# Five moves in the instruction order of a chunkwise mLSTM with an MLP on one core: sums, scans and x of two early steps, one weight chunk, and the low parts of the fourth tile

## The chip, the core and the metric

The kernel runs on one core of a Trainium2 chip. A core has five engines that run side by side, each with its own queue of instructions, which it takes in order: TensorE (PE) for matrix products, with its weight loads shown apart (PEld), VectorE (DVE), ScalarE (ACT), GpSimd (POOL), and SyncE (SP), which here does nothing but issue transfers (DMAs). The metric is the device time of one execution in microseconds (us). 

## What is computed

The reference is a recurrent attention layer (mLSTM) over 4 batches, 8 heads, 768 positions and 40 values a head, and an MLP over the 3072 tokens that come out, cut here to its core:

```python
for t in range(S):
    m_new = np.maximum(f_gate[:, :, t] + m, i_gate[:, :, t])
    f_stab = np.exp(f_gate[:, :, t] + m - m_new)
    i_stab = np.exp(i_gate[:, :, t] - m_new)
    C = f_stab * C + i_stab * (v_t outer k_t)
    n = f_stab * n + i_stab * k_t
    y[:, :, t] = sigmoid(o_t) * (C @ q_t) / max(|n . q_t|, 1)
x = y as tokens (3072 x 320)
h = x @ w_in                       # 320 x 2048
g = max(h, 0) + log1p(exp(-|h|))   # softplus
out = g @ w_out                    # 2048 x 320
```

The weights arrive as pairs of 32-bit words (float64) and are turned into float32 on the chip.

## The kernel before

**Steps and tiles.** The recurrence is worked in chunks of 128 positions. A chunk of one batch with its 8 heads is a *step*; there are 24, in the order of the list ORDER (line 35): the first chunks of all four batches as steps 0 to 3, then batch 0's chunks 1, 2 and 3 as steps 4, 5, 6, and so on. Three steps make a *tile* of 384 tokens, and there are 8 tiles, counted from 0. Names carry batch and chunk: x0_1 is x of batch 0, chunk 1 (step 4), pw0_2_0 the first half (4 heads) of step 5's decay matrix, X1 the tokens of tile 1; loq3 belongs to tile 3, the fourth.

**A step.** Steps 0 to 2 are written out in `first_tile`, steps 3 to 5 are run by `plain_step` (line 770), steps from 6 on by `wide_step` (line 832). The pieces of a step 3 to 5, in the order of the data: `decay`, a scan on DVE that makes the matrix of decays pw of four heads (L447), from factors fb that SP loads; `last_decays` (gw, L469) and `state_values` on POOL (vw, L475); `scores` (L517): PE's products of k and q into sp (L522), which DVE multiplies into pw (L524); `inter` (L543): the old state by q (ip, L546) and DVE's y1 (L549); `state` (cp, L499) and `new_state` (cn, L504); `values` (L553): PE's yp (L556), DVE's sum yy of yp and y1 (L560), its denominator nq (L562 to L564), POOL's product of the gate sig by it (L565), and DVE's x (L568); last `split_x` (L627): PE turns x over into xp (L633, L635), ACT casts it to a high part in X (L637), and DVE writes the low part (L639). `values` is a generator that is resumed by next(v): the first pieces up to POOL's product stand in the loop of `plain_step`, x is next(v) of line 823. From step 6 on the pieces have wide forms: iq (L575) and y (L578) on DVE, yq (L586), y again (L591), the transfer yd (L598), its reads yx and nw (L602 to L606), which POOL issues, and X.

**High and low parts.** PE multiplies in a rounded format, so operands are split into a high part (a cast) and a low part (the rest). For tiles from 2 on `prepare` (line 282) loads q and k of the three steps, ACT casts the high parts (hiq, hik, L300), and POOL makes the low parts (loq, lok) in two pieces of four heads each (L306). After each piece the generator waits for a number of products from the list PSY (L307, L309), [8, 12]: 8 for tile 2, 12 for later ones. SP then copies parts to the operands of a step: high parts by `load` (L391), low ones by `load_low` (L405), into qst and kst.

**Weights.** 16 chunks, eight (u, 0) of w_in and eight (u, 1) of w_out, each 256 of the 2048 columns or rows, run through `single` (line 204): two ACT instructions (mago or magi L212, sgo or sgi L215), two on DVE (L217, L219), then a cast to the high part on ACT (wih L250, woh L265) and the low part on POOL (wil L257, wol L267). `convert` (line 887) spaces these by the lists CW and CO, counted from a start that lines 1066 to 1072 set.

**The products.** For each tile and each of 16 blocks of 128 columns PE does 8 products hp (L1005, 384 columns), ACT two softplus passes (gh L877, hp L878), DVE the low part gl (L881), and PE, two blocks later, 9 products po (L971, 320 columns). ob (L1030, L1049) takes the results out; ob0h is a half result of tile 0, which is summed in two halves. X of a tile must be whole before its first hp block.

**What sets the order.** The products are written out in a fixed row, and everything else is put between them by a heap of generators (`start`, `resume`, `tick`, lines 917 to 940). A generator yields the number of products, counted from its own base, after which it wants to go on; a yield of -1000 - r means r products from now. For steps 3 to 5 these numbers are N_LOAD to N_XP (line 276), with bases 0, 40 and 76, for later steps W_LOAD to W_FIN (line 272). So a number smaller by 4 puts a piece four products sooner in the row of every engine that it uses. `in_order` (line 111) then pins on each engine the order in which the instructions were written. Small PSUM tiles (sp, cp, ip, yp, xp and their wide forms) take turns in two buffers (`Pair`, line 69), so the order of their use also sets who waits for whose buffer.

## Time and profile before

| | |
|---|---|
| median of three runs | 483.1 us (482.81 to 484.28) |
| the profiled execution | 484.25 us |
| span of its instructions in the trace | 482.5 us |
| TensorE busy | 466.4 us, 97% of the span |
| its weight loads, beside it | 445.2 us |
| VectorE busy | 325.0 us, 67% |
| ScalarE and GpSimd busy | 217.0 and 217.3 us, 45% each |
| mean clock granted to TensorE | 0.992 of full speed |

Busy time is time in which an engine had an instruction running; the span runs from the first instruction to the last. The profiled execution is one of its own, 1.15 us above the median of the runs, and 1.75 us of its time lie outside the span. In rows of the trace, a group of like instructions has its line, engine and operation, out<-in by the program's names with the numbers left out, shape and type of both, and how often it came (x); what stands in square brackets is the idle time of the engine just before, and the instruction or transfer that ended it ("issue" if the trace shows none). In a time line the first two columns are the start of a group in us and the time that it took. SPq and POOLq are the queues in which SP and POOL issue transfers.

### The profile page before, as it was taken

The numbers are of one execution on the slowest core, as the hardware profiler recorded it, in microseconds if no ns is written. First come the engines' busy times: TensorE is split into PE (matmuls) and PEld (weight loads), VectorE is DVE, ScalarE is ACT, GpSimd is POOL, SyncE is SP. The second block draws the span as 40 slices with busy tenths as digits, with TensorE's granted clock in tenths as the row PEclk, the third lists the DMA queues.
The fourth block names the chain that finished last, engine by engine and source line by source line (L and its number), as shares of the span: only waits on it lengthen the run. The fifth ranks groups of instructions, "written<-read, shape, count | busy, mean of one in ns | idle before, by whom it ended". The sixth has DMA issues, their size and how long they took to land.

```text
span 482.5 us, 9346 instructions
## 1 busy us (share of the span) xinstructions
PE 466.4 (97%) x3444; PEld 445.2 (92%) x3444; DVE 325.0 (67%) x517; ACT 217.0 (45%) x424; POOL 217.3 (45%) x303
## 2 busy tenths in 40 slices
PE   8999988998998999999999999999999999999996
PEld 7978887988898999999999999999999999999996
DVE  8879978778767768658757858767857856542121
ACT  1657536475744534354424434353425433334232
POOL 8366467477675145534275146525275244200000
PEclk9999998999999999999999999999999999999999
DMA  6957975789967984768667874669657461001001
GB/s 173 282 153 250 228 220 173 195 211 298 189 190 218 243 252 118 184 189 217 175 165 195 216 224 122 176 201 213 169 168 205 126 221 39 20 20 43 0 1 41
DMA packets 45607, 81.10 MB, mean 168 GB/s; under 512 B 6626, under 2 KB 23482, under 8 KB 45562
## 3 DMA queue, kind: packets, MB, share of 16 engines
q1 hardware_dynamic: 38218, 68.80, 52.1%
q0 software_dynamic: 4320, 8.26, 6.8%
q10 hardware_dynamic: 3024, 3.44, 2.1%
q8 instruction: 27, 0.44, 0.4%
q14 instruction: 18, 0.15, 0.1%
HBM read 52.38 MB, written 8.80 MB: 127 GB/s over the span
## 4 chain that ended last, share of the span: by engine, by line
PE 74%; DMA 13%; DVE 8%; issue 2%; SPq 2%; ACT 1%; DVEq 0%
PE hp L1005 32%; PE po L971 31%; PE yq L586 3%; DMA fb<-fz_d 3%; DMA wr<-in_w_in 3%; PE sp L522 3%; DVE pw L447 2%; PE cp L499 2%; DMA qst<-hiq 2%; PE iq L575 2%; DMA y<-fc_d 1%; DMA kst<-in_qk 1%; DMA sgp<-og 1%; DMA qst<-in_qk 1%; DVE sgo L219 1%
## 5 line engine op out<-in xcount | busy, mean ns | idle before, releaser
L1005 PE MATMUL hp<-X,wih 128*128 128x384 f32 x768 | 181.7, 341 | 0.4 <-ACT X L637 0.4
L877 ACT ACTIVATE gh<-hp 128x384 fp32r<-128x384 f32 x128 | 62.6, 489 | 160.0 <-PE hp L1005 142.2
L1005 PEld LDWEIGHTS hp<-X,wih 128*128 128x128 f32 x768 | 132.6, 189 | 2.2 <-issue 0.9
L881 DVE TENSOR_TENSOR gl<-hp,gh 128x384 fp32r<-128x384 f32 x128 | 70.1, 548 | 57.1 <-ACT hp L878 56.9
L971 PE MATMUL po<-woh,gh 128*128 128x320 f32 x384 | 83.7, 316 | 1.2 <-ACT ob0h L1030 1.2
L971 PE MATMUL po<-woh,gl 128*128 128x320 f32 x384 | 83.8, 313 | 0.0
L971 PE MATMUL po<-wol,gh 128*128 128x320 f32 x384 | 83.0, 316 | 0.0
L447 DVE TENSOR_TENSOR_SCAN pw<-fb,ident 128x512 f32<-128x512 f32 x48 | 72.4, 1545 | 4.1 <-DMA fb<-fz_d 3.6
L1005 PE MATMUL hp<-X,wil 128*128 128x384 f32 x256 | 69.1, 343 | 0.0
L971 PEld LDWEIGHTS po<-woh,gh 128*128 128x128 f32 x384 | 65.9, 190 | 2.3 <-ACT ob0h L1030 1.5
L971 PEld LDWEIGHTS po<-wol,gh 128*128 128x128 f32 x384 | 62.5, 190 | 1.6 <-issue 1.2
L971 PEld LDWEIGHTS po<-woh,gl 128*128 128x128 f32 x384 | 63.0, 189 | 0.3 <-issue 0.2
L878 ACT ACTIVATE hp<-hp 128x384 f32<-128x384 f32 x128 | 62.2, 486 | 0.0
L598 POOL DMA_DIRECT2D yd<-y x36 | 20.8, 578 | 90.4 <-DVE y L591 89.2
L1005 PEld LDWEIGHTS hp<-X,wil 128*128 128x128 f32 x256 | 45.8, 188 | 1.1 <-issue 1.0
L578 DVE TENSOR_TENSOR y<-iq,y 41x512 f32<-41x512 f32 x36 | 24.5, 682 | 29.5 <-PE iq L575 28.6
L522 PEld LDWEIGHTS sp<-qst,kst 120*128 120x128 f32 (+1 forms) x240 | 32.2, 191 | 5.7 <-issue 1.9
L522 PE MATMUL sp<-qst,kst 120*128 120x128 f32 (+1 forms) x240 | 33.1, 271 | 4.0 <-issue 1.7
L475 POOL TENSOR_TENSOR vw<-vt,gw 128x328 f32<-128x328 f32 x19 | 16.2, 854 | 39.3 <-DVE gw L469 27.5
L524 DVE TENSOR_TENSOR pw<-sp,pw 128x512 f32<-128x512 f32 x48 | 32.1, 682 | 1.7 <-PE sp L522 1.3
L623 ACT CAST X<-eg 128x384 fp32r<-128x384 f32 x18 | 9.2, 513 | 52.2 <-DVE eg L621 52.2
L504 DVE TENSOR_TENSOR cn<-cn,cp 40x328 f32<-40x328 f32 x16 | 7.8, 486 | 31.1 <-POOL cn L490 29.6
(131 smaller groups left out, 593.7 us busy)
## 6 DMA issues: line engine op xcount, KB each, us to landing
fb<-fz_d SPq DMA_DIRECT2D x42, 256.0 KB
vt<-in_vko SPq DMA_DIRECT2D x23, 324.0 KB
qst<-hiq SPq DMA_DIRECT2D x36, 160.0 KB
kst<-hik SPq DMA_DIRECT2D x36, 160.0 KB
wo<-in_w_out SPq DMA_DIRECT2D x8, 640.0 KB
wr<-in_w_in SPq DMA_DIRECT2D x8, 512.0 KB
eg<-in_oT SPq DMA_DIRECT2D x6, 576.0 KB
yd<-y POOLq DMA_DIRECT2D x36, 96.0 KB, 3.5
```

The lines of the kernel that those rows point to most:

```text
L447: nc.vector.tensor_tensor_scan(pw.rearrange(flat), fb.rearrange(flat), ident4.rearrange(flat), 0.0, ALU.mult, ALU.add)
L475: nc.gpsimd.tensor_tensor(z.vw, v1, z.gw.broadcast_to([128, H, E]), op=ALU.mult)
L522: nc.tensor.matmul(sp[:, j, :], z.kst[:, h, :], z.qst[:, h, :], start=True, stop=True)
L524: nc.vector.tensor_tensor(z.pws[i], sp, z.pws[i], op=ALU.mult)
L578: nc.vector.tensor_tensor(y, iq, y, op=ALU.mult)
L586: nc.tensor.matmul(yq[e0:e1, p, :], z.via[:, h * E : h * E + e1 - e0], z.pws[h // HG][:, h % HG, :], start=True, stop=True)
L598: nc.gpsimd.dma_start(rows[i], z.y[i * PP : i * PP + EP])
L877: nc.scalar.activation(gh, hp, AF.Softplus)
L878: nc.scalar.activation(hp, hp, AF.Softplus)
L881: nc.vector.tensor_tensor(gl, hp, gh, op=ALU.subtract)
L971: nc.tensor.matmul(po[j], a[:, j * 128 : (j + 1) * 128], w[:, f, :], start=(first and left[j] == 2), stop=(last and left[j] == 0),)
L1005: nc.tensor.matmul(hp, a, r, start=(i == 0), stop=(i == len(seq) - 1))
```

## The change

The edits, in the order of the diff:

- N_X and N_XP, the counts at which x is made and turned over, get one value for each of steps 3, 4 and 5. For step 3 x goes from 60 to 54 and now stands ahead of the parking of the state, its xp stays at 80; for step 4 x goes from 60 to 56 and xp from 72 to 64; step 5 keeps 60 and 72.
- PSY gets a value of its own for tile 3: 5 products between low parts in place of 12.
- In `split_x` the spacing of the cast and the low part behind xp becomes 2 and 3 products for step 3 and 1 and 1 for steps 4 and 5; before it was 2 and 3 for steps 3 and 4, and 1 and 1 for step 5.
- In `plain_step` the scan of the second half, before done apart for step 4 alone, is done apart for steps 4 and 5, and its place is now given as a count. For step 5 the first half's scan comes behind the matrix products of the first scores, just ahead of the product that reads it, and not ahead of them.
- The state copy of step 8 (`stack`, cs, L323 and L324) is due 12 products later, its scans 14 later (-30 to -16).
- The last piece of w_out chunk 6 (its low part) is due at 25 in place of 22 and w_in chunk 5 starts 9 products later.

The order of SP's instructions stays the same. Lines behind 784 of the kernel stand 8 further on in the changed one: L971, L1005 and L881 of the kernel before are L979, L1013 and L889 there.

```diff
--- before.py
+++ after.py
@@ -274,7 +274,7 @@
         -48, -34, -64, -8, 19, 8, 4, 6, 14, 17, 31, 47, 50, 62, -12, 68, 79, 107, 139,
     )
     N_LOAD, N_FB, N_SCAN, N_CN, N_VW, N_SIG, N_SP0, N_SP1, N_CP, N_CD, N_IP, N_VI, N_YP, N_X, N_XP = (
-        -20, -22, 9, 26, 12, 12, 12, 24, 40, 44, 45, 30, 46, 60, 72,
+        -20, -22, 9, 26, 12, 12, 12, 24, 40, 44, 45, 30, 46, (54, 56, 60), (80, 64, 72),
     )
     OF = [0, 8]
     N_PARK = 57
@@ -304,9 +304,9 @@
             for h in range(0, H, 4):
                 h2 = slice(h, h + 4)
                 nc.gpsimd.tensor_tensor(lo[:, h2], lo[:, h2].bitcast(F32), hi[:, h2], op=ALU.subtract)
-                yield -1000 - PSY[t > WIDE]
-
-    PRD, PSY = [62, 38, 78], [8, 12]
+                yield -1000 - PSY[min(t - WIDE, 2)]
+
+    PRD, PSY = [62, 38, 78], [8, 5, 12]
 
     parts = {}
     Xs = {}
@@ -633,9 +633,9 @@
             nc.tensor.transpose(xp[:, j, :], z.x[:, j * L : (j + 1) * L], ident)
         for j in range(2):
             nc.tensor.matmul(xp[j * 64 : (j + 1) * 64, 2, :], z.x[:, 2 * L :], ident, start=True, stop=True)
-        yield 1 if z.s == NH - 1 else 2
+        yield 2 if z.s == NG else 1
         nc.scalar.copy(X[:, 0:3, ts], xp)
-        yield 1 if z.s == NH - 1 else 3
+        yield 3 if z.s == NG else 1
         nc.vector.tensor_tensor(X[:, 3:6, ts], xp, X[:, 0:3, ts], op=ALU.subtract)
 
     def new_x(t):
@@ -776,19 +776,27 @@
             load(z)
             yield N_FB
             decays(z)
-        split = z.s == NG + 1
+        split = z.s > NG
         first = (0,) if split else (0, 1)
-        yield N_SCAN
-        decay(z, first)
-        yield N_VW
-        last_decays(z, first)
-        if z.s > NG and not split:
-            state_values(z)
+        if z.s < NG + 2:
+            yield N_SCAN
+            decay(z, first)
+            yield N_VW
+            last_decays(z, first)
         yield N_SIG
         out_gate(z)
         yield N_SP0
-        yield from rel(scores(z, 0))
+        p = scores(z, 0)
+        r = next(p)
+        if z.s < NG + 2:
+            yield -1000 - r
+        else:
+            yield N_SP0 + 3
+            decay(z, first)
+            last_decays(z, first)
+        next(p, None)
         if split:
+            yield N_SP0 + (3, 5)[z.s - NG - 1]
             decay(z, (1,))
             last_decays(z, (1,))
             state_values(z)
@@ -816,12 +824,12 @@
             if not r:
                 break
             yield -1000 - r
+        yield N_X[z.s - NG]
+        next(v)
         if z.s == NG:
             yield N_PARK
             next(c)
-        yield N_X
-        next(v)
-        yield N_XP + 8 * (z.s == NG)
+        yield N_XP[z.s - NG]
         yield from rel(split_x(z))
 
     def rel(g):
@@ -849,7 +857,7 @@
         if not last:
             ev += [(W_CN, lambda: old_state(z)), (W_VW, lambda: last_decays(z)), (W_VW, lambda: state_values(z))]
         if z.c > 0:
-            ev += [(W_CS, lambda: stack(z))]
+            ev += [(W_CS + 12 * (z.s == NH + 2), lambda: stack(z))]
         ev += [(W_SP0, lambda: scores(z, 0)), (W_SP1, lambda: scores(z, 1))]
         if not last:
             ev += [(W_CP, lambda: state(z)), (W_CP + 6, lambda: next(c)), (W_CD + 6, lambda: next(c))]
@@ -867,7 +875,7 @@
                 yield from rel(r)
 
     SOON = {NH + 1: (-96, -54), NH + 2: (-66, -58)}
-    SCAN = {NH + 1: -30, NH + 2: -30}
+    SCAN = {NH + 1: -30, NH + 2: -16}
     AWAY = 18
 
     def activation(t, f, hp, put):
@@ -886,7 +894,7 @@
 
     def convert(u, i):
         g = (weights_out if i else weights)(u)
-        for w in (CO[:4] + [16, 21] if (u, i) == (0, 1) else CO[:4] + [23, 23] if (u, i) == (1, 1) else CO if i else CW[:5] + [22] if u == 1 else CW[:3] + [9, 10, 26] if u == 2 else CW):
+        for w in (CO[:4] + [16, 21] if (u, i) == (0, 1) else CO[:4] + [23, 23] if (u, i) == (1, 1) else CO[:5] + [25] if (u, i) == (6, 1) else CO if i else CW[:5] + [22] if u == 1 else CW[:3] + [9, 10, 26] if u == 2 else CW):
             yield w
             next(g, None)
 
@@ -1068,7 +1076,7 @@
                 at = (-8, -4)[k]
             else:
                 at = (17 - 2 * 34, 26 - 34 + 6 * (u == 4))[i] + 34 * u if u < SPLIT // 2 else (168, 198)[i] + 48 * (u - SPLIT // 2)
-            start(convert(u, i), at - 21 * ((u, i) == (4, 1)))
+            start(convert(u, i), at - 21 * ((u, i) == (4, 1)) + 9 * ((u, i) == (5, 0)))
             start(fetch(i), at)
         start(first_states(), 0)
         LEAD, TS = 174, 16 * 17
```

## The prediction

> **What bounds the kernel now.** I read the busy time by stretches first, then the waits of TensorE (PE), then the time line of each engine around the two longest of them.
>
> The stretches (us, then each engine's busy time, the granted clock, the DMA share, GB/s):
>
> ```profile
> 152.00:478.00 326.00, 326.00 (x2396) 315.75 (x2395) 201.75 (x328) 132.98 (x268) 121.81 (x189) 1.00 0.54 148
> ```
>
> From 152 to 478 us PE is busy for 326.00 of 326 us, and nothing that the change moves lies there. What PE gains or loses before 152 us therefore moves the end by as much. PE's waits, longest first:
>
> ```profile
> PE yp L556 <- DVE X L639: 1.8, 1, 1.8
> PE sp L522 <- issue: 1.7, 1, 1.7
> PE cp L499 <- POOL vw L475: 1.3, 1, 1.3
> PE sp L522 <- DVE yy L560: 1.2, 1, 1.2
> PE po L971 <- ACT ob0h L1030: 1.2, 1, 1.2
> ```
>
> These five are 7.2 us. The change reorders something ahead of each of them, so 7.2 us would be the naive gain. The question is which of them the end hangs on. Two more stretches lose time without a wait, and a third shows the DMA engines:
>
> ```profile
> 58.11:61.53 3.42, 3.42 (x22) 3.03 (x21) 2.43 (x4) 2.26 (x5) 0.51 (x1) 0.50 1.03 255
> 82.00:85.42 3.42, 3.42 (x14) 3.42 (x13) 2.90 (x7) 1.57 (x3) 1.59 (x3) 0.50 0.39 132
> 88.00:135.00 47.00, 43.93 (x327) 41.62 (x324) 35.01 (x49) 30.40 (x56) 30.64 (x37) 1.00 0.90 227
> ```
>
> Twice PE runs 3.42 us at a granted clock of 0.50, which takes 1.7 us from it each time. From 88 to 135 us the DMA engines are busy to 0.90: there the loads, not PE, set the pace. The last wait is the 1.7 us "issue" one. The time line of SP, which issues the loads, and of PE shows it:
>
> ```profile
> 140.57 0.37 SPq L420 DMA_DIRECT2D vt<-in_vko  x1
> 144.07 0.74 SPq L405 DMA_DIRECT2D kst<-lok  x1
> 144.86 0.73 SPq L405 DMA_DIRECT2D qst<-loq  x1
> ```
>
> ```profile
> 142.93 1.09 PE L586 MATMUL yq<-pw,vi 128*64 128x128 f32 x16
> ...
> 150.46 0.63 PE L522 MATMUL sp<-qst,kst 120*128 120x128 f32 x4 [1.69 <-issue]
> ```
>
> The scores of the fourth tile's first step start at 150.46, 5.6 us after SP issued the second of the two loads of low parts that they read; PE had been ready at 150.46 - 1.69 = 148.77.
>
> **The change, part by part, from the end backwards.**
>
> *Low parts closer together.* What GpSimd (POOL) does around them, before and after; loq3 and lok3 are the low parts of q and k of tile 3 (the fourth), cs is the state copy of step 8, yx and nw are reads for step 7.
>
> ```order
> L306 TENSOR_TENSOR loq3_1478<-loq3_1478,hiq3_1572 120x512
> L324 TENSOR_TENSOR cs0_5_1602<-cn0_4_1418,cs0_5_1602 120x336
> L306 TENSOR_TENSOR loq3_1478<-loq3_1478,hiq3_1572 120x512
> L602 DMA yx0_4_1643<-yd0_4_1575 128x2x128
> L604 DMA yx0_4_1643<-yd0_4_1575 64x128 x2
> L606 DMA nw0_4_1647<-yd0_4_1575 128x1x128
> L306 TENSOR_TENSOR lok3_1480<-lok3_1480,hik3_1582 120x512 x2
> ```
>
> ```order
> L306 TENSOR_TENSOR loq3_1478<-loq3_1478,hiq3_1572 120x512 x2
> L306 TENSOR_TENSOR lok3_1480<-lok3_1480,hik3_1582 120x512
> L324 TENSOR_TENSOR cs0_5_1625<-cn0_4_1418,cs0_5_1625 120x336
> L306 TENSOR_TENSOR lok3_1480<-lok3_1480,hik3_1582 120x512
> L602 DMA yx0_4_1645<-yd0_4_1575 128x2x128
> L604 DMA yx0_4_1645<-yd0_4_1575 64x128 x2
> L606 DMA nw0_4_1649<-yd0_4_1575 128x1x128
> ```
>
> The last lok3 piece overtakes four DMA issues. ScalarE's (ACT) and POOL's times for these:
>
> ```profile
> 134.59 1.05 ACT L300 CAST hik<-lok 120x1024 fp32r<-120x1024 f32 x1 [2.44 <-DMA lok<-in_qk]
> ```
>
> ```profile
> 133.65 1.36 POOL L306 TENSOR_TENSOR loq<-loq,hiq 120x512 fp32r<-120x512 f32 x1
> 136.97 0.92 POOL L324 TENSOR_TENSOR cs<-cn,cs 120x336 fp32r<-120x336 f32 x1 [1.96 <-ACT cs L323]
> 137.85 1.34 POOL L306 TENSOR_TENSOR loq<-loq,hiq 120x512 fp32r<-120x512 f32 x1
> ```
>
> New sum: both loq pieces from 133.65 to 136.35; lok's first, whose high part is there at 134.59 + 1.05 = 135.64, to 137.7; cs 0.92 to 138.6; lok's last to 140.0. Before, the loads went out at 144.07. Now SP is what holds them: it issues vt until 140.57 + 0.37 = 140.94, so they go at about 141.0 and 141.8, 3.1 us sooner. At the same 5.6 us they land at 147.3, before PE's 148.77: the 1.69 us wait goes, with 1.4 us to spare. The cost: cs is 0.7 us later (its reader is the iq product, which the bound below covers), and the reads of yx and nw are under 1 us later; those feed X of tile 2, which no PE work before 152 us reads. I put both at nothing.
>
> *Steps 4 and 5, chunk conversion, scans of step 8: what they give PE.* Of the five waits, the POOL and ob0h ones (1.3 and 1.2) lie between 97 and 120 us; the new orders (step 7's values ahead of the w_out chunk, the w_in chunk later) remove what each waited for. PE then runs ahead by up to 2.5 us, but not to the end. ACT casts hik at 134.59 because its load has only landed then, and everything that ACT and the vector engine (DVE) do for PE stands behind it. DVE's y products, which follow in that order:
>
> ```profile
> 142.10 1.39 DVE L578 TENSOR_TENSOR y<-iq,y 41x512 f32<-41x512 f32 x2
> ```
>
> The first ends at 142.10 + 0.70 = 142.80, and PE's yq starts at 142.93: no slack. So PE cannot pass 142.93 sooner than hik allows, and 2.5 us of lead is handed back there. At 150.46 the end moves by -1.69 + S, where S is the shift of hik's load. That load stands at the end of SP's queue of 88 to 135 us, in unchanged order. So S is the shift of the queue's head, which is a pair of low-part loads too, of tile 2:
>
> ```profile
> 85.27 2.95 POOL L306 TENSOR_TENSOR lok<-lok,hik 120x512 fp32r<-120x512 f32 x2
> ```
>
> ```profile
> 88.25 0.73 SPq L405 DMA_DIRECT2D kst<-lok  x1
> ```
>
> *Sums and x in front of scans.* The pieces before lok on POOL follow DVE's order, which is the heart of the change. DVE between 63 and 76 us, before and after (names as in the kernel: pw a scan of step 5, yy the sum of step 4, x its output, sgi and sgo weight chunks; order prints a scan as L447 SCALAR_TENSOR_TENSOR):
>
> ```order
> L447 SCALAR_TENSOR_TENSOR pw0_2_0_803<-fb0_2_0_689,ident4_79 128x512
> L447 SCALAR_TENSOR_TENSOR pw0_2_1_805<-fb0_2_1_691,ident4_79 128x512
> L469 TENSOR_TENSOR gw0_2_819<-gT_93,pw0_2_0_803 128x4
> L469 TENSOR_TENSOR gw0_2_819<-gT_93,pw0_2_1_805 128x4
> L560 TENSOR_TENSOR yy0_1_833<-yp0_1_808,y10_1_746 128x328
> ...
> L217 SCALAR_TENSOR_TENSOR sgi4_790<-wr4_618,sgi4_790 128x640
> L524 TENSOR_TENSOR pw0_2_0_803<-sp0_0_2_826,pw0_2_0_803 128x512
> L219 SCALAR_TENSOR_TENSOR sgi4_790<-magi4_788,sgi4_790 128x640
> L568 TENSOR_TENSOR x0_1_863<-yy0_1_833,sig0_1_668 128x8x40
> ```
>
> ```order
> L560 TENSOR_TENSOR yy0_1_824<-yp0_1_804,y10_1_746 128x328
> ...
> L447 SCALAR_TENSOR_TENSOR pw0_2_0_832<-fb0_2_0_691,ident4_79 128x512
> L469 TENSOR_TENSOR gw0_2_834<-gT_93,pw0_2_0_832 128x4
> L524 TENSOR_TENSOR pw0_2_0_832<-sp0_0_2_817,pw0_2_0_832 128x512
> L217 SCALAR_TENSOR_TENSOR sgi4_790<-wr4_618,sgi4_790 128x640
> L447 SCALAR_TENSOR_TENSOR pw0_2_1_843<-fb0_2_1_693,ident4_79 128x512
> L469 TENSOR_TENSOR gw0_2_834<-gT_93,pw0_2_1_843 128x4
> L568 TENSOR_TENSOR x0_1_853<-yy0_1_824,sig0_1_668 128x8x40
> L219 SCALAR_TENSOR_TENSOR sgi4_790<-magi4_788,sgi4_790 128x640
> ```
>
> The sum overtakes both scans, x overtakes one weight instruction, and (not shown) X, the cast of x, now comes before y and L219 of sgo3. DVE's and ACT's times:
>
> ```profile
> 64.97 3.61 DVE L447 TENSOR_TENSOR_SCAN pw<-fb,ident 128x512 f32<-128x512 f32 x2 [1.68 <-DMA fb<-fz_d]
> ...
> 71.33 0.81 DVE L219 SCALAR_TENSOR_TENSOR sgi<-magi,sgi 128x640 uint32<-128x640 uint32 x1
> 72.06 1.29 DVE L568 TENSOR_TENSOR x<-yy,sig 128x320 f32<-128x320 f32 x1
> ...
> 75.40 1.73 DVE L219 SCALAR_TENSOR_TENSOR sgo<-mago,sgo 128x640 uint32<-128x640 uint32 x1
> 78.96 0.56 DVE L639 TENSOR_TENSOR X<-xp,X 128x384 fp32r<-128x384 f32 x1 [1.84 <-ACT X L637]
> ...
> 80.30 1.32 DVE L217 SCALAR_TENSOR_TENSOR sgo<-wo,sgo 128x640 uint32<-128x640 uint32 x1
> 81.66 1.79 DVE L219 SCALAR_TENSOR_TENSOR sgo<-mago,sgo 128x640 uint32<-128x640 uint32 x1
> 83.38 0.49 DVE L560 TENSOR_TENSOR yy<-yp,y 128x328 f32<-128x328 f32 x1
> ```
>
> ```profile
> 77.16 0.73 ACT L265 CAST woh<-sgo 128x640 fp32r<-128x640 f32 x1 [0.37 <-DVE sgo L219]
> 77.79 0.77 ACT L212 ACTIVATE mago<-wo 128x640 f32<-128x640 f32 x1
> 78.47 0.46 ACT L637 CAST X<-xp 128x384 fp32r<-128x384 f32 x1
> 78.83 0.78 ACT L215 ACTIVATE sgo<-wo 128x640 uint32<-128x640 uint32 x1
> ```
>
> sgi's L219 ended at 72.14; x ahead of it adds 1.2 us (71.33 to 72.06 is a slot's pitch, so 1.29 less the overlap), less up to 0.6 if the sum starts before 64.97, where DVE used to idle. ACT hands that delay on to sgo3, and X adds 0.5 to 0.9 (0.56, and it may wait for ACT). So sgo3's L219, once done at 77.13, is 1.1 to 2.1 later; I take 1.5, at 78.6, nearest to x and X without a wait. ACT's next three instructions now have no X among them: 79.61 - 77.16 less 0.36 is 2.1, so sgo4 is there at 80.7, where DVE's L217 took it up at 80.30. From there DVE works without a gap to step 5's sum at 83.38, so S = +0.4. Ends: if L219 ran at its other time, 0.81 in place of 1.73, S would be -0.5; at 2.1, +1.0.
>
> *The new wait.* xp, the transposition of x, now stands three hp products earlier on PE and ip behind it. PE's rows:
>
> ```profile
> 70.39 0.85 PE L1005 MATMUL hp<-X,wih 128*128 128x384 f32 x4
> ```
>
> Without the 1.2 us wait for yy PE has those three products done at 69.7 (70.39 + 3 x 0.17 - 1.2); x ends at about 72.4 (72.14 + 1.2 less 0.6 and less L219's 0.73 would be 72.0, without the 0.6 it is 72.6). So PE gets a new wait of 2.4 to 3.0 us at xp, where 1.2 and 1.8 go. It costs the end nothing while PE stays ahead of DVE's 83.8 at step 5's sum: PE's work of 70.9 to 77.9 (yp, at 79.67 less its 1.8 wait) fits behind 72.4 to 79.4, yp itself is 1.9, so 81.3 leaves about 2 us.
>
> *Sum.* -1.69 + 0.4 = -1.3. The profiled execution took 484.25 us (span 482.5): 482.95. The median of the runs is 483.1: **481.8**. Its own range, from S and from PE's 148.77: 480.9 to 482.6.
>
> **The rivals.**
>
> *Two windows at half clock.* Both windows at 0.50 follow a stretch with waits of PE under 2 us, and the new wait is longer and sits in the same part of the kernel. One window (1.7 us) disappears in the 2 us of room; two take 3.4, so S is 1.4 more and the end is where it was: 483.1.
>
> *Slower: the clock stays at half.* From three windows between 68 and 84 us on, PE and not DVE sets step 5's sum: 5.1 - 2 = 3.1 more, -1.3 + 3.1 = +1.8, 484.9. For it: waits at xp and then at ip, on top of each other. Against it: PE was busy through both half-clock windows of the trace (3.42 of 3.42), and each lasted one window only.
>
> The Trainium skill (TensorE: Matmul & The Clock Gate, Part 1, on oscillation) holds that the clock falls back only after a gap of over about 3.4 us without matmuls; by that neither kernel has such a window, and both these rivals have no chance. The trace disagrees, with 0.50 after waits of at most 1.8 us, so I leave them theirs.
>
> *More than forecast.* The same L219 takes 0.81 and 1.73 us, L568's x 1.29: DVE's times vary by what runs beside it. If two of the long ones shorten, S is -1.4 and low parts and PE both come sooner: -3.1 at most, about 480.3. That hik's load follows its queue's head one for one speaks for it; that POOL's work stays the same against.
>
> **How the numbers follow.** Forecast 0.52, two windows 0.18, slower 0.12, more 0.18. A difference of 0.3%, 1.45 us, is about what a measurement of this kernel can tell from none. The forecast lies near that line, so I split it in halves: faster 0.26 + 0.18 = 0.44; within 0.26 + 0.17 = 0.43; slower 0.13. The range leaves out the slower rival and the far end of the last: 480.1 to 483.8.
>
> **What would show it.** Right: the 1.69 us before the tile-3 scores is under 0.6; the pair of loads of low parts goes out 2 to 3 us sooner; PE waits over 2 us at L633 for x near 70 us, and near 136 us for ACT's gh behind hik; hik starts within 0.6 us of 134.6. Wrong: hik's cast a microsecond or more away from 134.6 either way, three slices of half clock between 68 and 84 us, or a wait of PE after 152 us.

## The result and the profile after

| | before | changed |
|---|---|---|
| median of 11 runs, us | 482.81 (480.6 to 484.28) | 485.88 (484.19 to 487.58) |
| ratio | | 1.0066 [1.0046, 1.0086] |
| the profiled execution, us | 484.25 | 487.58 |
| its span, us | 482.5 | 485.9 |
| mean granted clock | 0.992 | 0.986 |

The changed kernel is slower, by 0.66% or 3.2 us of 482.8, where 481.8 was forecast and 480.1 to 483.8 was the range. Both profiles lie high among the runs of their kernels: 487.58 is the highest of the eleven, and 484.25 is 1.4 us above the median. TensorE's waits in the changed kernel, longest first (total, times, longest); the line left out is a wait of 2.1 us at the very start, which the kernel before has too and the prediction's list leaves out as well:

```profile
PE xp L633 <- DVE x L568: 3.5, 2, 2.9
PE cp L499 <- DVE pw L524: 3.2, 1, 3.2
...
PE po L979 <- DVE gl L889: 1.8, 2, 1.0
PE cp L499 <- issue: 1.1, 1, 1.1
PE yq L586 <- DVE y L578: 0.9, 2, 0.7
```

None of the five waits of before (7.2 us together) is left among those of 0.5 us or more, so the edits moved what they were meant to move. But the five above come to 10.5, and four of them have DVE behind them. The stretches at a granted clock of 0.50, and the last part of the kernel:

```profile
70.48:80.72 10.24, 9.33 (x44) 7.97 (x45) 6.30 (x10) 6.58 (x12) 7.65 (x9) 0.50 0.54 170
121.68:125.09 3.41, 3.41 (x20) 3.33 (x18) 1.68 (x4) 3.17 (x8) 2.40 (x4) 0.50 0.92 225
152.00:485.00 333.00, 329.00 (x2413) 318.18 (x2411) 206.05 (x336) 135.29 (x273) 121.61 (x189) 1.00 0.53 147
```

Before had two windows of 3.42 us at half clock; now there are three on end, which begin within the new wait for x (68.51 to 71.39), and one behind the wait of 3.2. Where PE stands against before, from the start of the same hp products in both traces (after minus before, us):

| before's time | 29 | 70 | 77 | 85 | 99 | 117 | 122 | 139 | 146 | 154 | 191 | end |
|---|---|---|---|---|---|---|---|---|---|---|---|---|
| shift | -0.6 | -2.6 | +4.4 | +1.2 | -0.7 | +0.1 | +3.4 | +2.6 | +4.0 | +2.0 | +3.3 | +3.3 |

Read it as a story in three parts. PE is 2.6 ahead where the new order begins, loses 7 at xp and half clock, and has it all back at 99. Then 3.4 are lost at one place near 120 and are never made up. Of the 4.0 at 146, 2.0 come back by 154, where before had its 1.69 wait, and 1.3 go again around a wait at 194.

The place near 120. On DVE in the changed kernel, L217 is one half-step of a weight chunk, L524 the product that cp waits for:

```profile
115.87 4.61 DVE L217 SCALAR_TENSOR_TENSOR sgi<-wr,sgi 128x640 uint32<-128x640 uint32 x1
120.40 0.68 DVE L524 TENSOR_TENSOR pw<-sp,pw 128x512 f32<-128x512 f32 x1
```

and POOL beside it, with the issue of yd (L598) at the head of its row:

```profile
114.60 1.32 POOL L598 DMA_DIRECT2D yd<-y  x2
115.88 0.80 POOL L475 TENSOR_TENSOR vw<-vt,gw 128x328 f32<-128x328 f32 x1
116.58 1.62 POOL L267 TENSOR_TENSOR wol<-sgo,woh 128x640 fp32r<-128x640 f32 x1
118.10 0.94 POOL L324 TENSOR_TENSOR cs<-cn,cs 120x336 fp32r<-120x336 f32 x1
...
119.00 0.79 POOL L490 TENSOR_TENSOR cn<-cn,flast 40x328 f32<-40x328 f32 x1
```

The same instruction in the kernel before:

```profile
115.67 0.81 DVE L217 SCALAR_TENSOR_TENSOR sgi<-wr,sgi 128x640 uint32<-128x640 uint32 x1
```

L217 has no idle time ahead of it and the same size as before; it runs from 115.87 to 120.48, and POOL's row without a pause runs from 114.60 to 119.79. It got through 0.7 us after the row was over. The second such place, where the low parts have been moved together, DVE first (the L610 held here is that of step 6; the one of step 7 follows at 148.69, and neither waits for its data):

```profile
138.20 3.95 DVE L610 SCALAR_TENSOR_TENSOR nm<-nw 128x128 f32<-128x128 f32 x1
...
148.69 0.28 DVE L610 SCALAR_TENSOR_TENSOR nm<-nw 128x128 f32<-128x128 f32 x1
```

and POOL, again with yd's issue at the head:

```profile
134.93 1.15 POOL L598 DMA_DIRECT2D yd<-y  x2 [2.08 <-DVE y L591]
136.06 2.59 POOL L306 TENSOR_TENSOR loq<-loq,hiq 120x512 fp32r<-120x512 f32 x2
138.58 1.30 POOL L306 TENSOR_TENSOR lok<-lok,hik 120x512 fp32r<-120x512 f32 x1
139.83 0.91 POOL L324 TENSOR_TENSOR cs<-cn,cs 120x336 fp32r<-120x336 f32 x1
140.71 1.28 POOL L306 TENSOR_TENSOR lok<-lok,hik 120x512 fp32r<-120x512 f32 x1
...
143.72 0.59 POOL L606 DMA_DIRECT2D nw<-yd  x1
```

In the kernel before:

```profile
137.51 0.53 DVE L610 SCALAR_TENSOR_TENSOR nm<-nw 128x128 f32<-128x128 f32 x1
```

L610 ends at 142.15, POOL's last low part at 141.99. PE's waits for gl (0.81 at 144.84) and y (0.21 at 146.93) follow it:

```profile
144.84 0.56 PE L979 MATMUL po<-woh,gl 128*128 128x320 f32 x2 [0.81 <-DVE gl L889]
...
146.93 1.09 PE L586 MATMUL yq<-pw,vi 128*64 128x128 f32 x16 [0.21 <-DVE y L578]
```

### The profile page after: what moved, and what is told of

It reads as the page before. It is cut to its first block, busy times and chain, and to the rows that moved or that the text cites. A ratio compares the mean times of both kernels' runs of the same rounds, so it can differ in the third digit from the quotient of the medians.

```text
span 485.9 us, 9355 instructions
## 1 busy us (share of the span) xinstructions
PE 467.9 (96%) x3444; PEld 446.8 (92%) x3444; DVE 329.6 (68%) x517; ACT 216.8 (45%) x424; POOL 219.3 (45%) x303
## 4 chain that ended last, share of the span: by engine, by line
PE 62%; DMA 13%; DVE 13%; ACT 4%; POOL 4%; issue 3%; SPq 1%; ACTq 0%; DVEq 0%; POOLq 0%
PE hp L1013 27%; PE po L979 26%; PE yq L586 3%; DMA wr<-in_w_in 3%; PE sp L522 2%; DVE pw L447 2%; PE cp L499 2%; DVE sgi L217 2%; DMA yd<-y 1%; DMA nw<-yd 1%; DMA vt<-in_vko 1%; DMA fb<-fz_d 1%; PE iq L575 1%; DMA sgp<-og 1%; DMA kst<-in_qk 1%
## 5 line engine op out<-in xcount | busy, mean ns | idle before, releaser
L1013 PE MATMUL hp<-X,wih 128*128 128x384 f32 x768 | 182.1, 341 | 0.4 <-ACT X L637 0.4
L1013 PEld LDWEIGHTS hp<-X,wih 128*128 128x128 f32 x768 | 132.7, 189 | 2.5 <-issue 1.2
L889 DVE TENSOR_TENSOR gl<-hp,gh 128x384 fp32r<-128x384 f32 x128 | 70.2, 549 | 59.1 <-ACT hp L886 58.9
L979 PE MATMUL po<-woh,gl 128*128 128x320 f32 x384 | 84.2, 314 | 1.8 <-DVE gl L889 1.8
L979 PE MATMUL po<-woh,gh 128*128 128x320 f32 x384 | 83.5, 316 | 0.0
L979 PE MATMUL po<-wol,gh 128*128 128x320 f32 x384 | 83.0, 316 | 0.1
L447 DVE TENSOR_TENSOR_SCAN pw<-fb,ident 128x512 f32<-128x512 f32 x48 | 70.6, 1506 | 0.0
L1013 PE MATMUL hp<-X,wil 128*128 128x384 f32 x256 | 69.6, 345 | 0.0
L979 PEld LDWEIGHTS po<-woh,gh 128*128 128x128 f32 x384 | 65.9, 190 | 0.8 <-ACT cn L506 0.3
L979 PEld LDWEIGHTS po<-woh,gl 128*128 128x128 f32 x384 | 63.1, 190 | 2.6 <-DVE gl L889 2.3
L979 PEld LDWEIGHTS po<-wol,gh 128*128 128x128 f32 x384 | 62.6, 190 | 1.4 <-issue 1.0
L598 POOL DMA_DIRECT2D yd<-y x36 | 20.8, 579 | 91.8 <-DVE y L591 86.8
L1013 PEld LDWEIGHTS hp<-X,wil 128*128 128x128 f32 x256 | 46.1, 189 | 1.1 <-issue 1.0
L524 DVE TENSOR_TENSOR pw<-sp,pw 128x512 f32<-128x512 f32 x48 | 31.9, 681 | 0.5
```

Of the source, the lines that this page charges most:

```text
L447: nc.vector.tensor_tensor_scan(pw.rearrange(flat), fb.rearrange(flat), ident4.rearrange(flat), 0.0, ALU.mult, ALU.add)
L524: nc.vector.tensor_tensor(z.pws[i], sp, z.pws[i], op=ALU.mult)
L598: nc.gpsimd.dma_start(rows[i], z.y[i * PP : i * PP + EP])
L889: nc.vector.tensor_tensor(gl, hp, gh, op=ALU.subtract)
L979: nc.tensor.matmul(po[j], a[:, j * 128 : (j + 1) * 128], w[:, f, :], start=(first and left[j] == 2), stop=(last and left[j] == 0),)
L1013: nc.tensor.matmul(hp, a, r, start=(i == 0), stop=(i == len(seq) - 1))
```

## The experiments

In the expectations theory A is that POOL's closed-up rows hold DVE's two-operand instructions; B, that the edits on steps 3 to 5 cost through the new wait and the half clock; H, which came later, that only a row behind a transfer issued by POOL holds them to its end. A hold is an instruction that runs longer than its usual time with no wait ahead of it. All ratios are to the kernel before, in runs on the same chip; e9 to e13 are single executions with a profile and have none.

| run | what it is | ratio | 95% interval |
|---|---|---|---|
| e1_steps | edits on steps 3 to 5 alone | 1.0035 | 1.0017 to 1.0054 |
| e2_rest | all the others | 1.0038 | 1.0013 to 1.0062 |
| e3_low_back | change without the low parts | 1.006 | 1.0036 to 1.0084 |
| e4_wol_back | change without (6, 1) | 1.0057 | 1.0038 to 1.0075 |
| e5_fill | e1, PE filled ahead of xp | 1.0024 | 0.9995 to 1.0052 |
| e6_low | low parts alone | 1.0061 | 1.0033 to 1.009 |
| e7_wol | (6, 1) alone | 1.0007 | 0.9984 to 1.003 |
| e8_win_step8 | (5, 0) and step 8 alone | 1.0021 | 0.9991 to 1.005 |
| e14_yd_act | change, yd of steps 6 and 7 issued by ACT | 1.0126 | 1.009 to 1.0163 |
| e15_xp_later | e1, step 4's xp later | 1.0019 | 0.9997 to 1.0041 |
| e16_finish_later | e6, step 7's finish later | 0.9984 | 0.9966 to 1.0003 |
| e17_after_finish_later | change, finish of steps 6 and 7 later | 1.0022 | 0.9997 to 1.0047 |
| e18_finish_alone | before, step 7's finish later | 0.9991 | 0.9967 to 1.0014 |

**The change in two halves.** e1 is the changed kernel with these lines as in the kernel before, e2 the kernel before with these lines as changed:

```diff
-                yield -1000 - PSY[t > WIDE]
+                yield -1000 - PSY[min(t - WIDE, 2)]
-    PRD, PSY = [62, 38, 78], [8, 12]
+    PRD, PSY = [62, 38, 78], [8, 5, 12]
-            ev += [(W_CS, lambda: stack(z))]
+            ev += [(W_CS + 12 * (z.s == NH + 2), lambda: stack(z))]
-    SCAN = {NH + 1: -30, NH + 2: -30}
+    SCAN = {NH + 1: -30, NH + 2: -16}
...
+ ... CO[:4] + [23, 23] if (u, i) == (1, 1) else CO[:5] + [25] if (u, i) == (6, 1) else CO if i else ...
...
+            start(convert(u, i), at - 21 * ((u, i) == (4, 1)) + 9 * ((u, i) == (5, 0)))
```

> Only the edits of steps 3 to 5 (sums, x, xp, scans); low parts, weight chunks and step 8 as before. Theory A (the loss is DVE being held by rows of POOL instructions without a gap, at 115.9 and 138.2 us): both places are as before, L217 of sgi near 116 us takes under 2 us and L610 near 138 us under 0.6 us; the time is within 0.7 us of before. Theory B (the loss is the wait for x at xp near 70 us and the half clock behind it, 10.2 us long in the changed kernel): that wait of 2.4 to 3 us is there and with it three windows at half clock, and the kernel is 2 to 3 us slower than before.

> Everything but the edits of steps 3 to 5. Theory A: most of the loss is here, 2 to 3 us over before, with an L217 of 3 us or more near 116 us or an L610 of 3 us or more near 138 us. Theory B: no wait at xp near 70 us, and the time is that of before or, by the 1.7 us wait at the fourth tile's scores that goes, up to 1.7 us less.

Both cost, and about the same: 0.35% and 0.38%, together 0.73% where the whole has 0.66%. So neither theory has the whole loss on its side: e1 is 1.7 us over before, where A had under 0.7 and B 2 to 3, and e2 1.8, where A had 2 to 3 and B nothing. In e1 the stretch behind the wait for x is there as in the change:

```profile
71.00:81.24 10.24, 9.93 (x51) 8.49 (x51) 5.69 (x9) 7.01 (x12) 7.88 (x9) 0.50 0.52 165
```

In e2 it is not (two single windows of 3.4, as before), but step 6's L610 took 3.43 us.

**One edit taken out.** e3 is the change with PSY as before, e4 with the last low part of w_out chunk 6 back at 22:

> The changed kernel with the fourth tile's low parts spaced by 12 products again. Theory A: L610 near 138 us falls from 3.95 to under 0.6 us and PE's waits of 0.8 and 0.2 us for gl and y behind it go; the wait of 1.7 us at the scores near 150 us is back; so 0.5 to 1 us slower than the changed kernel, and L217 near 116 us still takes over 3 us. Theory B: L610 does not matter; 1.7 us slower than the changed kernel.

> The changed kernel with the low part of w_out chunk 6 (wol) ahead of step 7's vw on POOL again, as before; nothing else in the row of any engine moves. Theory A: L217 of sgi near 116 us falls from 4.61 us to under 2 us, PE's wait at cp from 3.2 us to about 1.3, the half-clock window near 122 us goes; 2 to 3.5 us faster than the changed kernel, so near before. Theory B: within 0.7 us of the changed kernel.

By their ratios neither returns more than half a microsecond, with intervals that lie on the whole's own; A had 2 to 3.5 us for e4, and both theories had e3 slower than the changed kernel. In e3 L610 was not held and L217 was (4.61 us); in e4 L217 took 0.81, the half clock near 122 was gone, and L610 was held (3.79). So in these single profiles each hold goes with the edit that was named for it, but taking one away does not bring its microseconds back.

**One edit alone.** e6 has the PSY lines of the diff above, e7 the one of (6, 1), e8 the other three; e5 is e1 with ten products of the identity in step 4's xp, written over by what follows:

```diff
+        if z.s == NG + 1:
+            for j in range(10):
+                nc.tensor.matmul(xp[:, j % 2, :], ident, ident, start=True, stop=True)
```

> The kernel with the edits of steps 3 to 5 alone (e1_steps), and ten products of the identity by itself (0.275 us each in the profile's rows of such products) in front of step 4's xp, in the PSUM tile that xp then overwrites: PE works through the 2.9 us in which it waited for x. Theory B (the wait of 2.9 us brings the three windows at half clock, and they are what these edits cost): no half clock between 68 and 84 us, or one window, and 1 to 1.5 us faster than e1_steps, so the time of before. Rival (the half clock follows from something else, such as the work before it): three windows at half clock as in e1_steps, and its time.

> The kernel before with the fourth tile's low parts closer together and nothing else. Theory A (POOL's instructions without a gap hold DVE's instructions with two SBUF operands): one of DVE's L610, L613 or L621 between 137 and 142 us takes 2 us or more where it took 0.6, and PE has a new wait of 0.5 to 1.2 us for gl or y behind it; the 1.7 us wait at the scores near 150 us goes; time within 0.7 us of before. Theory of the prediction: no new wait, 1.7 us less than before.

> The kernel before with one swap on POOL: step 7's vw ahead of the low part of w_out chunk 6. Theory A: L217 or L219 of sgi near 116 us meets POOL's vw, wol, cs, cn in a row; if POOL starts first, it takes 4 us or more, and the kernel is 1 to 3 us slower than before; if DVE starts first (in the profile of before it starts 0.3 us ahead of POOL's wol), the 1.3 us wait for vw at cp goes and the time is up to 1.3 us less. Theory of the prediction: 0 to 1.3 us less.

> The kernel before with the later start of w_in chunk 5 and the later scans and state copy of step 8, and nothing else. From the sum of the runs so far (all edits but those of the steps cost about 2 us, wol back saves 1.4 and low parts back 0.4) some 0.5 us slower than before is left for these; theory A has no held instruction of over 2.5 us on DVE between 95 and 150 us, PE's wait of 1.2 us for ob0h is gone. Theory of the prediction: 0 to 1.2 us less than before.

e7 is a clear miss for theory A's price. Its profile has L217 held for 4.63 us and PE's cp waiting 2.2, and the time of its runs is that of before:

```profile
114.23 4.63 DVE L217 SCALAR_TENSOR_TENSOR sgi<-wr,sgi 128x640 uint32<-128x640 uint32 x1
```

e8 holds another instruction, L625 (3.65), where A had none over 2.5, at no price that its interval shows. e5 took the wait at step 4's xp from 2.9 to 0.2, with one of 0.85 at ip behind it, and the half clock from 10.2 us to 6.8, in which PE never stood:

```profile
74.49 2.53 PE L546 MATMUL ip<-cn,qst 128*128 128x42 f32 x16 [0.85 <-DVE pw L524]
```

```profile
75.70:82.50 6.80, 6.80 (x37) 6.39 (x37) 3.92 (x7) 4.76 (x8) 5.90 (x6) 0.50 0.57 176
```

B had one window at most, and 1 to 1.5 us back; e5's 1.0024 can't be told from e1's 1.0035. And e6 costs about as much as the whole change, without one hold of over 2 us in its profile. Something else works there. Its edit puts both pieces of lok ahead of step 7's reads of yx and nw, and step 7's L610 now waits for nw:

```profile
146.85 0.29 DVE L610 SCALAR_TENSOR_TENSOR nm<-nw 128x128 f32<-128x128 f32 x1 [3.08 <-DMA nw<-yd]
```

This profile (482.76 us) is of one of the four runs of e6 under 484 us; e9 and e10 look at that place again.

**Before and low parts once more.** e9 is the kernel before, e10 is e6:

> The kernel before once more, for a second profile: does each execution have the waits on which the prediction's sum stands? If the 1.7 us wait at the scores near 150 us belongs to the kernel (theory of the prediction), it is here again, 1 us or more. If it belongs to the one execution that was profiled, which at 484.25 us was 1.7 us over the median of 482.5, it is under 0.6 us here when the time is near or under the median.

> The kernel before with the low parts closer together once more. Its twelve times fell into two groups, four at 482.3 to 483.7 us and eight at 485.5 to 488.4, and the profile was of the first group. Theory A: in the slower group one of L610, L613 and L621 near 138 us is held by POOL for 2.5 us or more, and PE is 2 to 4 us later from there on. Rival (the slower group is of the clock): a half-clock stretch of 6 us or more before 152 us, and no held instruction.

The time lines of POOL, DVE and PE, put in one, of the kernel before in its second profile (479.67 us):

```profile
135.12 0.74 POOL L602 DMA_DIRECT2D yx<-yd  x1 [0.17 <-issue]
...
136.89 0.59 POOL L606 DMA_DIRECT2D nw<-yd  x1
137.46 2.57 POOL L306 TENSOR_TENSOR lok<-lok,hik 120x512 fp32r<-120x512 f32 x2
...
142.06 0.28 DVE L610 SCALAR_TENSOR_TENSOR nm<-nw 128x128 f32<-128x128 f32 x1
...
145.98 0.56 PE L522 MATMUL sp<-qst,kst 120*128 120x128 f32 x4
...
146.58 2.33 DVE L447 TENSOR_TENSOR_SCAN pw<-fb,ident 128x512 f32<-128x512 f32 x2
```

and with the low parts closer together (483.85 us):

```profile
136.46 3.18 POOL L306 TENSOR_TENSOR lok<-lok,hik 120x512 fp32r<-120x512 f32 x2
...
141.37 0.59 POOL L606 DMA_DIRECT2D nw<-yd  x1
...
147.45 0.29 DVE L610 SCALAR_TENSOR_TENSOR nm<-nw 128x128 f32<-128x128 f32 x1 [4.39 <-DMA nw<-yd]
...
150.44 0.41 PE L971 MATMUL po<-woh,gl 128*128 128x320 f32 x1 [0.81 <-DVE gl L881]
...
150.97 2.33 DVE L447 TENSOR_TENSOR_SCAN pw<-fb,ident 128x512 f32<-128x512 f32 x2
...
154.67 0.78 PE L499 MATMUL cp<-vw,vt 128*40 128x41 f32 x16 [1.55 <-POOL vw L475]
```

The read of nw goes out 4.5 us later (1.6 of that because the cast of hik began later in this execution, 131.90 against 130.33; the other 2.9 are, but for some tenths, the two pieces of lok ahead of it). Step 7's L610 then stands 4.39 us on DVE for its data, and what is queued behind it on DVE, gl and step 9's scans, with POOL's vw and PE's cp behind them, is late with it: PE waits 0.81 + 1.55, and e9 has no wait there. Neither answer expected of e10 came, no hold of POOL's and no half clock of 6 us, but at 483.85 us it is not one of the group from 485.5 us on either, so no profile shows that group. e9 shows a second thing. Its scores of tile 3 start without a wait. The 1.69 us that the forecast was to win were in the one profiled execution of before; all ten other profiles with the old PSY (e1, e3, e5, e7, e8, e9, e12, e13, e15 and e18) have 0.2 or none.

**Whether the read is the cost,** e16 tests: e6, with step 7's finish and end 16 products later, behind the scans. e18 is that alone, without the low parts:

```diff
-        d = AWAY + 30 * (z.s == NH)
+        d = AWAY + 30 * (z.s == NH) + 16 * (z.s == NH + 1)
```

> The low parts closer together alone (e6_low, 485.2 us in the mean), with step 7's L610, L611, L613 and L621, which need the reads nw and yx, 16 products later, behind step 9's scans on DVE. If the reads that come 4 us later hold DVE's queue and through it POOL's vw and PE's cp near 154 us: DVE does not wait for nw ahead of the scans, PE's wait of 1.3 to 1.6 us at cp near 154 us is gone, and the time is 1.5 to 2.7 us less than e6_low, 482.5 to 483.7 us. Rival (the cost of the low parts lies elsewhere): within 0.8 us of e6_low.

> The kernel before with step 7's L610 to L625 16 products later and nothing else. If the low parts closer together are worth something when DVE does not wait (the prediction had 1.7 us, the median of the second look at before about nothing): e16_finish_later is faster than this by 0.5 to 1.5 us, and this is at the time of before, 482.3 us within 0.6. Rival (the later finish alone is the gain): this is 481.3 us within 0.6, as e16_finish_later.

DVE in e16:

```profile
143.90 3.18 DVE L447 TENSOR_TENSOR_SCAN pw<-fb,ident 128x512 f32<-128x512 f32 x2
147.00 0.26 DVE L610 SCALAR_TENSOR_TENSOR nm<-nw 128x128 f32<-128x128 f32 x1
```

The scans go first and L610 waits for nothing. From e6's 1.0061 [1.0033, 1.009] to 0.9984 [0.9966, 1.0003], each against the kernel before on its own chip, is 0.77%, 3.7 us, more than the 1.5 to 2.7 expected: the cost of the low parts is gone whole. So it came through the place of step 7's finish on DVE, and in both profiles of this kernel what kept it there was the read of nw. Against e18 (0.9991) e16 gains nothing that can be told: low parts sooner are worth nothing that shows here, and in ten of eleven profiles with the old PSY next to nothing waited for them. The same cure on the changed kernel, with step 6's finish moved too:

```diff
-        d = AWAY + 30 * (z.s == NH)
+        d = AWAY + 30 * (z.s == NH) + 26 * (z.s == NH) + 16 * (z.s == NH + 1)
```

> The changed kernel with the L610 to L625 of step 6 later by 26 products and those of step 7 by 16, so that what PE waits for (gl, y, step 9's scans) stands ahead of them on DVE. If the loss between 136 and 160 us comes through them: PE's waits of 0.8 and 0.2 us for gl and y near 145 us go, and the time falls by 1 to 2.5 us from 485.9, to 483.4 to 484.9 us; what is left over before is that of the steps' edits (1.4) and of L217 near 116 us. Rival (PE is late there anyway by what came before 136 us): within 0.7 us of the changed kernel.

1.0022 [0.9997, 1.0047]: 0.44%, about 2.1 of the 3.2 us, come back, though L217 was held for 4.61 us in its profile too. PE has no wait left between 136 and 160 us. But e17 moves step 6's L610 away from POOL's row as well as step 7's from the late read, so it doesn't tell the two apart. What is left can be told neither from nothing nor from e1's cost.

**What holds DVE.** A second profile of the changed kernel, and two kernels with a block at the end that does nothing but put rows of POOL's tensor_tensor beside one DVE instruction; e13 puts none, one or two issues of a transfer on POOL ahead of the row:

```diff
+        def held(n, k, wait=False):
+            if k:
+                nc.gpsimd.tensor_copy(o[:, 2048:2056], p[:, 0:8])
+            for j in range(k):
+                nc.gpsimd.dma_start(scr[j], v[:, j * 384 : j * 384 + 384])
+            (pool_waits if wait else pool_row)(n)
+            after_first()
+            nc.vector.scalar_tensor_tensor(r, q, -1.0, q, op0=ALU.mult, op1=ALU.max)
+            gap()
+
+        held(5, 0)
+        held(5, 2)
+        held(3, 2)
+        held(5, 2, True)
+        held(5, 1)
+        held(5, 0)
```

> The changed kernel once more, for a second profile. Theory A: L610 near 138 us is again held for 3 us or more, and L217 near 116 us for over 4 us, and three windows at half clock follow xp near 70 us; the rival is that one or more of the three is a matter of the single execution and is not seen here.

> The kernel before with a probe behind its end: POOL does rows of TENSOR_TENSOR (128x512, some 1.3 us each in the traces) without a wait between them, and DVE, released by the end of the first of a row, does one instruction. Theory A, that a DVE instruction with two SBUF operands waits until POOL's whole row has ended: behind a row of five it takes some 5.2 us more than alone (0.28 us for 128x128), behind a row of three 2.6 us more; a reciprocal, with one operand, and a subtraction with one operand in PSUM take their usual 0.95 and 0.55 us; where each instruction of POOL waits for the one before it, the DVE instruction gets in and takes under 1.7 us. Rival, that POOL and DVE take turns instruction by instruction: at most 1.6 us in every row. In the last part DVE has six instructions of two operands in a row and POOL two: by theory A POOL waits for all six, by the rival for one.

> The kernel before with a second probe behind its end. Each part: POOL issues none, one or two DMAs and then does a row of three or five TENSOR_TENSOR (1.25 us each); DVE, released by the end of the row's first, does one SCALAR_TENSOR_TENSOR of 128x128 with two SBUF operands (0.29 us alone, 1.15 us in the first probe, which had no DMA issue). Theory H (behind a DMA issue POOL keeps DVE out until its first pause): 1.15 us without a DMA issue; some 4.9 us in a row of five and 2.4 us in a row of three behind two; 1.2 to 1.7 us where each POOL instruction waits for the one before it. Rival (what holds DVE is something else in the kernel): 1.15 us in all.

In e11 (488.15 us) L610 took 3.63 us and L217 1.11, and half clock came as two stretches of 6.8 us near 64 and 77 and one window near 146. So one of the three signs was there again, and the kernel was no faster for it: the holds come and go between executions. POOL's row near 119 in e11 shows why one went:

```profile
119.21 0.73 POOL L475 TENSOR_TENSOR vw<-vt,gw 128x328 f32<-128x328 f32 x1 [0.65 <-DVE gw L469]
```

POOL waited 0.65 us for gw between the issue of yd and the row, where in the first profile it had no pause. In e12 theory A fell. Beside rows of five or three the instruction took 1.15 us: it was held to the end of the POOL instruction then running, and then it was in. The reciprocal and the subtraction from PSUM took their usual 0.95 and 0.55. In e13 the six cases, in the order of the diff:

```profile
484.75 1.15 DVE L389 SCALAR_TENSOR_TENSOR vtp<-vtp 128x128 f32<-128x128 f32 x1
...
493.69 4.79 DVE L389 SCALAR_TENSOR_TENSOR vtp<-vtp 128x128 f32<-128x128 f32 x1
...
502.49 2.36 DVE L389 SCALAR_TENSOR_TENSOR vtp<-vtp 128x128 f32<-128x128 f32 x1
...
509.25 1.15 DVE L389 SCALAR_TENSOR_TENSOR vtp<-vtp 128x128 f32<-128x128 f32 x1
...
518.17 4.79 DVE L389 SCALAR_TENSOR_TENSOR vtp<-vtp 128x128 f32<-128x128 f32 x1
525.60 1.14 DVE L389 SCALAR_TENSOR_TENSOR vtp<-vtp 128x128 f32<-128x128 f32 x1
```

No issue ahead: 1.15. One issue or two, row of five: 4.79, to the row's end; row of three: 2.36. The fourth case has two issues too, but each POOL instruction writes over the one before and waits for it, and 1.15 is back. That is theory H, and e11's pause fits it. e14 takes the issue off POOL's row in the changed kernel:

```diff
-            nc.gpsimd.dma_start(rows[i], z.y[i * PP : i * PP + EP])
+            (nc.scalar if z.s in (NH, NH + 1) else nc.gpsimd).dma_start(rows[i], z.y[i * PP : i * PP + EP])
```

> The changed kernel, in which ScalarE issues the transfers yd of steps 6 and 7, not POOL; POOL's rows of vw, wol, cs, cn near 116 us and of the low parts near 137 us stay as they are, but follow no DMA issue. Theory H: L217 of sgi near 116 us takes under 2 us, L610 near 138 us under 1.6 us, and the kernel is 1.5 to 3 us faster than the changed one, so 483 to 484.5 us. Rival (the rows themselves hold DVE): both as before, 4 us or more, and the time within 0.7 us of the changed kernel.

L217 took 0.81 us and L610 0.93: both holds are gone. Only L610's is a test of H: POOL's row of five tensor_tensors stood there as in the change, without an issue ahead, and L610 was in at the end of the one then running. Near 120 POOL stood 3.11 us in its row for woh, and L217 came before the rest. The time rose all the same, where 1.5 to 3 us less was expected. ACT in e14:

```profile
117.57 1.68 ACTq L598 DMA_DIRECT2D yd<-y  x2
119.30 0.49 ACT L885 ACTIVATE gh<-hp 128x384 fp32r<-128x384 f32 x1 [3.30 <-issue]
```

ACT stands 3.30 us around the issue of yd, with gh queued behind it, and cp waits 2.9 us where it waited 3.2 in the change. The wait went to another queue. The y that yd reads was there at 114.74, so it is not what ACT waited for; what it was the trace doesn't name.

**Step 4's xp later**, e1 with its count at 72 in place of 64:

```diff
- ... 45, 30, 46, (54, 56, 60), (80, 64, 72),
+ ... 45, 30, 46, (54, 56, 60), (80, 72, 72),
```

> The edits of steps 3 to 5 alone (e1_steps), with step 4's xp at 72 as before, so behind step 5's ip and not ahead of it. If PE's wait at xp and the half clock behind it are what these edits cost: the 2.9 us wait at xp near 70 us falls to under 1 us, half clock lasts 6.8 us or less between 60 and 84 us, and the time is 1 to 2 us less than e1_steps, 482 to 482.9 us. Rival (it is the scans that come later, and DVE's order with them): PE waits elsewhere for DVE instead, at ip or yp near 75 us, and the time stays at 483.9 within 0.6.

The wait at step 4's xp fell from 2.9 to 1.9, now for pw, with one of 1.4 at yp in addition, and 10.2 us of half clock were left as well, in two stretches. So it took away neither the wait nor the half clock whose price it was to show. 1.0019 can't be told from e1's 1.0035, nor from 1.

## Why the prediction was wrong, point by point

**"At 150.46 the end moves by -1.69 + S": the base was one execution's.** The 1.69 us were read as a trait of the kernel. Ten other profiles have 0.2 or none there. In the profile of before the cast of hik had waited 2.44 us for its load, and POOL's low parts and SP's pair of loads came behind it; in e9 and e18 the cast begins at 130.3 and 130.4, not 134.59. That is not the whole of it: in e5 the cast began at 134.22 and the pair went out 0.15 us later than in before, and PE, there at 150.04, did not wait. The rest of the sum stood on this wait, so there was nothing to win.

**"The reads of yx and nw are under 1 us later; ... I put both at nothing": the term that cost most.** From the start of hik's cast to the read of nw it is 6.3 us in before (140.91 - 134.59) and 6.6 in e9; in e6 and e10 it is 9.5, in the changed kernel 8.5. So 2 to 3 us, where the step had them under one. And the price was looked for at the wrong reader: X of tile 2 is read after 152, but step 7's L610, which reads nw, stands in DVE's queue ahead of gl and the scans of step 9. For the low parts alone e6 against e16 puts that price at 3.7 us. In the whole change it is mixed with the hold of step 6's L610, which stands in the same queue: e17, which moves both, gives 2.1 of the 3.2 back, and how they share it stays open.

**"both loq pieces from 133.65 to 136.35": POOL's row was priced for POOL alone.** In before POOL stood 1.96 us ahead of cs, which parts its row from yd's issue; L610 began beside cs (137.51) and was in at its end. In the changed kernel the row stands right behind the issue, and L610 takes 3.95 us; at the other place L217 takes 4.61. This was in no rival. What it costs by itself is not settled: e7's profile has the hold and its time is 1.0007 [0.9984, 1.003], e4's lacks that of L217 and gains too little to tell. It is shown to stop DVE, not shown to be worth a given time.

**"It costs the end nothing while PE stays ahead of DVE's 83.8": not borne out by e1.** The wait was sized well (2.88 against 2.4 to 3.0), and DVE's sum came at 84.20:

```profile
84.20 0.49 DVE L560 TENSOR_TENSOR yy<-yp,y 128x328 f32<-128x328 f32 x1
```

The three windows of the slower rival happened (10.24 us at 0.50), yet the sum of step 5 was only 0.8 later than before, where that rival had 3.1 more. PE is at +1.2 at 85 and at -0.7 at 99. But e1 says that the edits on steps 3 to 5 cost 1.0035 [1.0017, 1.0054], 1.7 us, where this step had them at S alone, 0.4. Which part of that is the clock stays open, as e5 and e15 each took some of wait or clock away and neither can be told from e1.

**S, hik and the pair of loads.** SP's loads in the changed kernel, tile 2's and tile 3's:

```profile
89.06 0.74 SPq L405 DMA_DIRECT2D kst<-lok  x1
...
143.14 0.74 SPq L405 DMA_DIRECT2D kst<-lok  x1
```

S was +0.8 (88.25 to 89.06), forecast 0.4 and at most 1.0; hik's cast came 0.7 later. Both steps were right in size. The pair for tile 3 went 0.9 sooner, not 3.1: POOL's row began at 136.06, 2.4 us later than forecast, lok was ready at 141.99, and SP's vt ahead of the pair ended at 143.03. That PE would run ahead and hand its lead back at hik never came up: PE was 2.6 us late there, after the hold near 116. One sum of the prediction is off: in "More than forecast" -3.1 from 483.1 is 480.0, not 480.3.

**Behind 152.** "Nothing that the change moves lies there" was said, and a wait of PE there was named as a sign of a mistake. It came, at 194 (the second profile of the changed kernel, e11, has none there):

```profile
194.00 0.70 PE L979 MATMUL po<-woh,gl 128*128 128x320 f32 x3 [1.01 <-DVE gl L889]
```

**The parts don't add.** Low parts alone cost 0.61%, the change without them 0.60%, the whole 0.66%. The edits load the same stretch of DVE and POOL between 115 and 155 us, and the profiles show one late piece hide another: step 7's L610 waits 3.1 and 4.4 us for nw in e6 and e10, where step 6's was not held, and 0 to 1.9 us in the changed kernel, e11, e2 and e4, where it was held for 3.4 to 4.0. No version beats the kernel before by more than its interval; the nearest is e16, 0.9984 [0.9966, 1.0003].

## What to carry to other kernels

When a piece is moved ahead of a transfer's issue, follow the transfer to the instruction that waits for it and read what is queued behind that instruction on its engine, not only who uses its result. A wait seen in one profile is a term of the sum only when a second execution of the same kernel has it. And a pause of GpSimd's behind a transfer's issue can be what lets a VectorE instruction in: look for those with two operands in SBUF beside it before closing it, though what that was worth here stays open.

## What the runs showed of the hardware

**VectorE behind a row of GpSimd's.** Counted over the 20 traces here: of DVE instructions with two operands in SBUF that started beside two or more of POOL's tensor_tensors in a row, with no transfer issued by POOL just ahead of the row, 157 were not held, and 289 took over 0.15 us more than usual; every one of these got in at the end of the POOL instruction then running. Where the row stood right behind a POOL transfer's issue, 8 of 9 were held to the end of POOL's tensor_tensors, rows of four or five; the ninth, in e7, got in after the first of two. The probe has the same with 1.15 against 4.79 us. The Trainium skill (SBUF — State Buffer, section "Who interferes with whom") says that a VectorE instruction with two SBUF inputs contends with a GpSimd instruction that reads SBUF, at a port pair that the two share, and, of VectorE's two-port modes, that whoever issues first has the pair for the whole instruction. By that a hold lasts one instruction of POOL's; the trace agrees for rows without an issue ahead of them and not for those behind one, where the hold spans the row. Why an issue makes the difference no run shows.

**Half clock behind short waits.** The granted clock fell to 0.50 for three windows on end (10.24 us) at a wait of 2.88 us, and for two (6.8 us) in e5, where the longest wait of PE in the 20 us ahead was 1.1 and PE was busy in all of the 6.80. The Trainium skill (TensorE: Matmul & The Clock Gate, Part 1, on oscillation) gives as the rule that PE has no idle gap of over about 3.4 us; no gap near these windows is that long, and the clock fell all the same.

**How far one kernel's executions lie apart.** Runs of the kernel before lie between 479.6 and 486.1 us, wider than what most of these edits are worth. The same kernel shows a hold or a wait for its loads in one execution and not in the next, so a single profile tells how a delay comes about, but not what it costs on the median.
